# A sparse-attention and MoE kernel: another order for the lead-in, finer weight pieces, batch 2's loads behind a gate

## The chip, the cores and the metric

One core of one Trainium2 chip. The metric is the device time of one execution in microseconds.

## What is computed

Four batches of 8 heads, 768 positions, 64 values a head. Every query sees the keys less than 16 positions away, and one key a block of 32 positions (the block's maximum, with the block's mean as its value):

```python
k_sum = k.reshape(B, H, nb, block, D).max(axis=3)
v_sum = v.reshape(B, H, nb, block, D).mean(axis=3)
scores_l = np.where(mask_l, scale * q @ k.T, -1e9)            # |i - j| < 16
scores_s = scale * q @ k_sum.T + np.log(block)
a = softmax(concatenate([scores_l, scores_s]))
x = a @ concatenate([v, v_sum])                               # -> (3072, 512)
h = x @ w_in                                                  # (512, 2048)
out = (h * sigmoid(1.702 * h)) @ w_out                        # (2048, 512)
```

Inputs and output are float32; the kernel works in bf16 and fp16 and accumulates in float32.

## The kernel before

The kernel runs as a sequence of stages on TensorE (PE), written out by hand; each engine's instructions keep the order of the program text.

**The lead-in** does the first half (384 positions) of batch 0's attention with a layout of its own. Keys of head pairs 0 and 1 come over SyncE's queue and are cast on ScalarE (`cast_k0`); all other loads are cast on the way and are issued by GpSimd, in the order of the text: queries of four heads at a time (`load_q0`), keys of pairs 2 and 3, values `v0n`, then w_in in five pieces, w_out in four (512 KB each in SBUF), and the late half of batch 0's queries (`load_q1`). Each of GpSimd's loads first waits for the landing of the eighth load before it. For each pair p the steps are: `k_turn` and `q_turn` (transposes on PE), `k_own` and `q_copy` (out of PSUM), `k_max` (block maxima `ks`, on VectorE), `s_bias` (a band of -30000 outside the window, as a product), `s_own` and `s_edges` (scores), `s_exp`; for two pairs at once `b_turn` and `b_exp` (block scores). `v_sum` forms block sums of values with products by shifted selector matrices `E`. `av_own`, `av_edges`, `av_blocks` multiply by the values, `v_norm` divides, `x_turn` and `x_copy` give the transposed x, and `ff_first` begins the first two column tiles of the first product. `idle` issues products whose result is not used.

**Stages behind it.** `ff_in(u)` multiplies half u of x by w_in, 128 columns at a time, and ScalarE applies the gelu into `gT`. `ff_out(u, ms, part)` multiplies by w_out, 128 tokens (`ms`) and four of the 16 row tiles at a time; its 12 slots are numbered, and tables `plan0` (batch 0's second half beside the first `ff_out`) and `plan1` (batch 1 beside the second) say which attention step follows which slot: q = `q_late`, t = `tq` (query transposes), s = `scores` (products and exp), m = `mask` (VectorE multiplies by the 0/1 mask `mk`), v = `values`, x = `tx`. Batches 1 to 3 then go through a loop in which the two products use seven block products instead of eight, on sums and differences of weights (`ws`, by `w_sum`) and of `gT` (`gs`).

**Loads of the batches.** `load_batch(b)` issues, on GpSimd, four key loads (192 KB each), twelve value loads (64 KB each) and the query loads of batch b. For batch 2 it stands in the text after slot 2 of the second `ff_out`; GpSimd gets to it whenever it has done what stands ahead. `value_rows(s)` copies halo rows of the values (SyncE's queue), sums them by blocks on PE (`vsum`, tile `ps_vs`) and spreads the sums (`vw<-vs`). `xk` and `xq` turn keys and queries by DMA on SyncE's queue.

Of the kernel before, what the change touches and what calls it, by code (L numbers as in the profile page):

```python
# [35 lines left out]
def kernel(  # L36
# [47 lines left out]
    RQ = 4  # L84
# [13 lines left out]
    def cast_k0(p):  # L98
        if p == 0:
            kb2[0] = castp2.tile([128, 4, RK, D], BF16, name="kb", tag="kb")  # L100
        act.activation(out=kb2[0][:, 2 * p:2 * p + 2].rearrange("p h r d -> p h (r d)"), in_=k0f[p], func=ACT.Copy)
# [82 lines left out]
    mk = consts.tile([128, NQ, QT], BF16, name="mk")  # L184

    def masks():
        pool.memset(mk[:, 2:4], 1.0)
        for par, own, blk, halo in ((0, 0, 64, 96), (1, 64, 0, 32)):
            mid = 2 + par
# [42 lines left out]
    def clear_values(eng, s):  # L232
        eng.memset(vw[s][96:128, 0], 0.0)
        eng.memset(vw[s][96:128, 0, :, D:VC], 1.0)
        eng.memset(vw[s][32:64, NQ - 1], 0.0)
        eng.memset(vw[s][32:64, NQ - 1, :, D:VC], 1.0)
# [25 lines left out]
    def load_w_out(c):  # L262
        wo = moe_w_out.rearrange("(nt ni) d -> ni nt d", ni=128)
        pool.dma_start(out=w_out_sb[:, c * 4:(c + 1) * 4, :],
                       in_=wo[:, c * 4:(c + 1) * 4, :])
# [32 lines left out]
    def idle(n, cols=128):  # L298
# [82 lines left out]
    def k_turn(p):  # L381
        ps = st["K", p] = pturn.tile([128, 1024], BF16, name="ps_k", tag="turn")
        o = 2 * (p % 2)
        turn_plain(ps[:, 0:S], kb2[p // 2][:, o:o + 2])
# [16 lines left out]
    def q_turn(p):  # L401
        if p % 2 == 0:
            st["Q2"] = pturn.tile([128, 1024], BF16, name="ps_q", tag="turn")
        st["Q", p] = st["Q2"][:, p % 2 * HALF:p % 2 * HALF + HALF]
        turn_plain(st["Q", p], qe[:, 2 * p:2 * p + 2])
# [11 lines left out]
    def q_late(p, eng):  # L417
        if p < 2:
            ps = psb.tile([128, 2048], BF16, name="ps_q", tag="big")
        else:  # L420
            ps = pmm.tile([128, 1024], BF16, name="ps_q", tag="mm")
        turn_plain(ps[:, 0:HALF], qb2["late"][:, 2 * p:2 * p + 2])
        copy(eng, qT[p][0][:, HALF:S].rearrange("p (c r) -> p c r", r=JH),
             ps[:, 0:HALF].rearrange("p (r c) -> p c r", r=JH))
# [58 lines left out]
    def v_sum(ps_):  # L483

        for p in ps_:
            if p == 0:
                t = pturn.tile([128, 512], F32, name="ps_vt", tag="turn")
                st["VT", 0], st["VT", 1] = t[:, 0:2 * D], t[:, 2 * D:4 * D]
                st["VT", 0, 1] = t[:, 0:4 * D]
            elif p > 1:  # L490
                st["VT", p] = pturn.tile([128, 512], F32, name="ps_vt", tag="turn")[:, 0:2 * D]
            for i in range(2):
                for j in range(NJ):
                    o = EX - (p % 2 * 2 + i) * 32 - 4 * j
                    pe.matmul(out=st["VT", p][:, i * D:(i + 1) * D], lhsT=E[:, o:o + 128],
                              rhs=v0n[:, 2 * p + i, j, 0:D],
                              start=(j == 0), stop=(j == NJ - 1), skip_group_check=True)

    def v_copy(ps_, eng):
        h0, n = 2 * ps_[0], 2 * len(ps_)  # L500
        copy(eng, vs4[:, h0:h0 + n, 0:D], st[("VT",) + ps_].rearrange("p (h d) -> p h d", d=D))
# [94 lines left out]
    def mask(half, p):  # L596
        a = a_sb[half, p]
        dve.tensor_mul(a, a, mk[:, half * TH:(half + 1) * TH, :].unsqueeze(1)
                       .to_broadcast([128, 2, TH, QT]))
# [269 lines left out]
    def ff_out(u, ms, part):  # L869
        if part == 0:  # L870
            po_now[ms] = pmm.tile([128, d_model], F32, name="po", tag="mm")
        po = po_now[ms]
        for nt in range(4 * part, 4 * part + 4):
            pe.matmul(out=po, lhsT=gT[u % 2][:, nt, ms * 128:(ms + 1) * 128],
                      rhs=w_out_sb[:, nt, :], start=(nt == 0), stop=(nt == NT - 1))
        if part == 3:
# [7 lines left out]
    gate3 = consts.tile([128, 2], F32, name="gate3")  # L884
    dve.memset(gate, 0.0)

    def gelu_soon():

        act.activation(out=gate[:, 1:2], in_=gate[:, 0:1], func=ACT.Gelu_apprx_sigmoid)
# [5 lines left out]
    dve.memset(warm, 0.0)  # L895
# [25 lines left out]
    bands()  # L921
    dve.memset(v0n[:, :, :, D:VC], 1.0)
    clear_sums(dve)
    dve.tensor_copy(out=ident16, in_=ident)
# [11 lines left out]
    s_bias(1)  # L936
    q_copy(0, dve)
    q_copy(1, dve)
    k_max(0)
    idle(8)  # L940
    s_own(0)
    s_own(1)
    s_edges(0)
    s_exp(0)
    s_edges(1)
    s_exp(1)
    k_max(1)
    k_turn(2)
    k_own(2, dve)
    b_turn(0)  # L950
    k_turn(3)
    k_own(3, act)
    b_exp(0)
    q_turn(2)
    q_turn(3)
    q_copy(2, dve)
    q_copy(3, dve)
    k_max(2)
    k_max(3)
    s_bias(2)  # L960
    s_bias(3)
    s_own(2)
    s_own(3)
    s_edges(2)
    s_exp(2)
    s_edges(3)
# [8 lines left out]
    av_edges(0)  # L975
# [5 lines left out]
    v_sum((2,))  # L981
    v_copy((2,), act)
# [4 lines left out]
    v_sum((3,))  # L987
    v_copy((3,), act)
# [11 lines left out]
    gelu_soon()  # L1000
    x_turn(3)
    ff_first(1)
    x_copy(3, dve)
    ff_first(2)
    ff_first(3)
# [7 lines left out]
    dve.memset(vw[0][:, :, :, D:VC], 1.0)  # L1013
# [11 lines left out]
    dve.memset(vw[1][:, :, :, D:VC], 1.0)  # L1025
# [69 lines left out]
    for i, (ms, part) in enumerate((ms, part) for part in range(4) for ms in range(JH)):  # L1095
        ff_out(0, ms, part)
        beside0(i)
        if i in (10, 11):
            w_sum(i - 10, 0)
            w_sum(i - 10, 1)  # L1100

    todo = {3: [lambda: tk(0, 1, act)], 4: [lambda: w_sum(2, 0)], 5: [lambda: tk(1, 1, act)],
            6: [lambda: w_sum(2, 1)], 7: [lambda: w_sum(3, 0)], 8: [lambda: tk(2, 1, act)], 
            10: [lambda: w_sum(3, 1)], 9: [lambda: tq(0, 1, dve)], 11: [lambda: tk(3, 1, act)], 12: [lambda: tq(1, 1, dve)],
# [8 lines left out]
    for i, (ms, part) in enumerate((ms, part) for ms in range(JH) for part in range(4)):  # L1113
        ff_out(1, ms, part)
        beside(1, i)
        if i == 2:
            load_batch(2)
# [5 lines left out]
    for b in range(1, B - 1):  # L1123
# [5 lines left out]
        for n in range(0, NT, 2):  # L1129
# [12 lines left out]
            if nxt:  # L1142
                if n == 0 and b > 1:
# [112 lines left out]
```

## Time and profile before

| | |
|---|---|
| Time, median of 3 runs | 205.96 us (205.91 to 206.78) |
| The profiled execution's own time | 205.39 us |
| Its span, first to last instruction | 203.4 us |
| PE / VectorE / ScalarE / GpSimd busy | 196.7 / 141.2 / 125.4 / 89.9 us |
| Mean granted PE clock | 0.998 |
| DMA packets moved | 28.13 MB, mean 138 GB/s |
| GpSimd's DMA queue (`software_dynamic`) | 69648 packets, 84.8% of 16 engines' span |

The busy times are unions of an engine's instructions. A matmul's end is modelled, so a full PE means that none of its waits is seen, not that it is at its peak. In a chain of waits each piece shows start, length and what was running; a DMA's time to landing runs from its issue. In tables by stretch the columns are the stretch, its length, the busy time of each engine with its count of instructions, the granted PE clock, the DMA engines' mean concurrency and the GB/s that they moved. Rows name instructions as engine, operation, out<-in, shape and count; all have line 28, that of a helper, so tiles tell them apart.

### The profile page before, as it was taken

What the parts mean: (1) busy time and instruction counts of PE and PEld (TensorE: products, weight loads), DVE (VectorE), ACT (ScalarE), POOL (GpSimd) and SP (SyncE); (2) the same over time, 40 slices, a digit from 0 to 9 for tenths busy, and PEclk for the clock granted to TensorE, in tenths of its full rate; (3) what the DMA queues carried; (4) which work ended last, traced back from release to release, by engine and by line L of the source; (5) the groups of instructions that cost most, each with busy time, mean ns of one, the idle gap of its engine ahead of it and who ended that gap; (6) DMA issues with size and microseconds to landing.
All of it is one profiled execution on the core that took longest, in us unless ns stands there. A gap on an engine that the chain in (4) does not pass through costs nothing.

```text
span 203.4 us, 5851 instructions
## 1 busy us (share of the span) xinstructions
PE 196.7 (97%) x2358; PEld 136.6 (67%) x2358; DVE 141.2 (69%) x391; ACT 125.4 (62%) x240; POOL 89.9 (44%) x141
## 2 busy tenths in 40 slices
PE   6889999999999999999999999999999999999993
PEld 5548655556754566655888876666888865578882
DVE  6586894694856884898767789896769567758221
ACT  4584976638786717777871446778670559984220
POOL 7964489447899584000986034000000009980000
PEclk9999999999999999999999999999999999999999
DMA  5999999999999999999999979999022930000223
GB/s 171 169 165 204 207 207 215 189 156 243 116 122 170 176 170 178 127 165 155 114 181 156 173 140 139 110 247 179 0 104 62 185 119 3 0 0 0 106 105 103
DMA packets 95994, 28.13 MB, mean 138 GB/s; under 512 B 83664, under 2 KB 93152, under 8 KB 95968
## 3 DMA queue, kind: packets, MB, share of 16 engines
q0 software_dynamic: 69648, 13.24, 84.8%
q1 hardware_dynamic: 26176, 14.39, 34.8%
q8 instruction: 18, 0.29, 0.6%
q10 hardware_dynamic: 144, 0.13, 0.2%
q14 instruction: 8, 0.07, 0.1%
HBM read 27.26 MB, written 6.29 MB: 165 GB/s over the span
## 4 chain that ended last, share of the span: by engine, by line
PE 91%; DMA 3%; DVE 3%; issue 1%; ACT 0%; POOLq 0%; DVEq 0%
PE ph L28 32%; PE poA L28 16%; PE po L28 11%; PE poB L28 7%; PE phA L28 4%; PE ps_av L28 4%; PE poC L28 4%; PE ps_s L28 3%; DMA qe<-in_q_dram 3%; DVE ks L28 2%; PE ps_t L28 1%; PE ps_x L28 1%; PE phC L28 1%; PE phB L28 1%; PE phE L28 1%; DVE qT L28 1%
## 5 line engine op out<-in xcount | busy, mean ns | idle before, releaser
L28 PE MATMUL ph<-xT,w_in_sb 128*128 128x384 f16 x400 | 67.8, 326 | 0.1
L28 PEld LDWEIGHTS <-w_in_sb 128*128 128x128 f16 x442 | 42.7, 98 | 27.2 <-issue 0.2
L28 ACT ACTIVATE gT<-ph 128x384 f16<-128x384 f32 x100 | 47.9, 491 | 18.4 <-PE ph L28 17.6
L28 PEld LDWEIGHTS <-gT 128*128 128x128 f16 x312 | 28.8, 98 | 11.3 <-issue 0.2
L28 ACT ACTIVATE a_sb<-ps_s 128x768 bf16<-128x768 f32 (+1 forms) x32 | 25.0, 826 | 12.0 <-PE ps_s L28 12.0
L28 PEld LDWEIGHTS <-gs 128*128 128x128 f16 x288 | 27.7, 98 | 3.4
L28 POOL DMA_DIRECT2D vw<-in_v_dram x36 | 24.6, 699 | 11.9 <-DMA kb<-in_k_dram 5.4
L28 POOL TENSOR_TENSOR gs<-gT 128x384 f16<-128x384 f16 x8 | 7.3, 911 | 43.3 <-ACT gT L28 43.2
L28 PE MATMUL po<-w_out_sb,gT 128*128 128x512 f16 x96 | 23.6, 380 | 0.0
L28 PE MATMUL poA<-ws,gs 128*128 128x256 f16 x144 | 18.7, 273 | 0.0
L28 DVE TENSOR_TENSOR a_sb<-a_sb,mk 128x768 bf16<-128x768 bf16 x28 | 14.9, 554 | 5.5 <-ACT a_sb L28 5.0
L28 DVE TENSOR_TENSOR x<-ps_av,rc 128x384 f16<-128x384 f32 x32 | 17.8, 557 | 1.1
L28 DVE TENSOR_TENSOR gs<-gT 128x384 f16<-128x384 f16 (+1 forms) x34 | 13.3, 390 | 7.2 <-ACT gT L28 6.9
L28 POOL DMA_DIRECT2D qb<-in_q_dram x16 | 15.1, 961 | 2.5 <-DMA w_in_sb<-in_moe_w_in_dram 1.2
L28 PEld LDWEIGHTS <-kx 64*128 64x128 bf16 (+1 forms) x378 | 9.9, 95 | 6.8 <-issue 3.6
L28 POOL DMA_DIRECT2D kb<-in_k_dram x14 | 13.6, 986 | 0.3 <-issue 0.3
L28 DVE TENSOR_REDUCE ks<-kx 128x24 bf16<-128x768 bf16 x12 | 11.4, 948 | 3.4 <-ACT kx L28 3.2
L28 ACT ACT_TABLE_LOAD x10 | 12.8, 1283 | 1.0 <-PEq L1240 0.8
L28 ACT ACTIVATE osb<-poA 128x256 f32<-128x256 f32 x9 | 3.5, 384 | 16.1 <-PE poA L28 16.1
L28 ACT ACTIVATE s<-poA 128x256 f32<-128x256 f32 x11 | 4.2, 385 | 11.2 <-PE poA L28 11.2
L28 PEld LDWEIGHTS <-a_sb 128*64 128x64 bf16 (+2 forms) x400 | 7.9, 108 | 2.8 <-issue 1.3
L28 PE MATMUL poA<-ws,gT 128*128 128x256 f16 x72 | 9.3, 273 | 0.0
(117 smaller groups left out, 288.2 us busy)
## 6 DMA issues: line engine op xcount, KB each, us to landing
out_dram<-osb SPq DMA_DIRECT2D x22, 256.0 KB, 3.9
kb<-in_k_dram POOLq DMA_DIRECT2D x14, 192.0 KB, 6.6
qb<-in_q_dram POOLq DMA_DIRECT2D x12, 192.0 KB, 10.5
vw<-in_v_dram POOLq DMA_DIRECT2D x36, 64.0 KB, 5.5
w_out_sb<-in_moe_w_out_dram POOLq DMA_DIRECT2D x4, 512.0 KB, 12.8
w_in_sb<-in_moe_w_in_dram POOLq DMA_DIRECT2D x3, 512.0 KB, 12.4
vw<-vs SPq DMA_DIRECT2D x6, 198.0 KB, 6.6
gT<-in_k_dram SPq DMA_DIRECT2D x2, 384.0 KB, 3.4
```

Source lines behind the costliest of these rows:

```text
L28: r = f(*a, **kw)
```

## The change

- The first four heads' queries come in two loads of two heads instead of one of four, and with three rows a partition (128 partitions) instead of four (96); the identity is built between them. Each pair's `q_turn` has its own PSUM tile.
- Keys of pairs 0 and 1 are cast into a layout that full 128 x 128 transposes can take.
- `idle`: 28, 4 and 8 bf16 products of 128 columns become 4 of 256 columns and 2 of 128 in float32.
- The block sums of the first four heads are one group of 6 products (`v_sum4`) with a second selector `E4`, then multiplied by a 0/1 tile `own`; `selectors` sets both tiles, and the clearing of `v0n`, `ks0` and `vs4` moves ahead of `bands`.
- The order of the lead-in: scores of a pair are followed at once by its edges and exp; `k_own(0)` moves from ScalarE to VectorE, `q_copy(3)` from VectorE to ScalarE; the first pair's products and `v_sum4` move ahead of `b_turn(1)`; `ff_first(1)` ahead of `x_turn(3)`.
- One mask of two tiles for all positions instead of one for every tile; rows outside the sequence are zero in `vw` now, the ones column too.
- w_in in seven pieces instead of five; w_out in eight (row tiles 0-2, 2-4, 4-6, 6-8, 8-12, 12-14, 14-16) rather than four, with the masks behind the third of them.
- The first `ff_out` takes two row tiles a step (24 slots); `plan0` is renumbered and `q_late` does two pairs at once. In `plan1` both t steps follow slot 2 and s02, s03 follow slot 3.
- `w_sum` moves later; its last two parts go into batch 1's loop.
- `load_batch(2)` stands after slot 3, and GpSimd first copies one column of the tile that the exp of pair 2 (s02) writes.

The diff, cut:

```diff
-    RQ = 4
+    RQ = 3
...
-    def load_q0(g):
-        pool.dma_start(out=qe[:, 4 * g:4 * g + 4].rearrange("p h r d -> p h (r d)"),
-                       in_=q[0, 4 * g:4 * g + 4, 0:HALF].rearrange("h (p r) d -> p h (r d)", r=RQ))
+    def load_q0(a, z):
+        pool.dma_start(out=qe[:, 2 * a:2 * z].rearrange("p h r d -> p h (r d)"),
+                       in_=q[0, 2 * a:2 * z, 0:HALF].rearrange("h (p r) d -> p h (r d)", r=RQ))
...
+    E4 = lead.tile([128, 20 + 128], BF16, name="E4")
+    own = lead.tile([128, 4, 1], F32, name="own")
-    warm = lead.tile([128, 512], BF16, name="warm")
+    warm = lead.tile([128, 256], F32, name="warm")
...
     def selectors():
         dve.memset(E, 0.0)
+        dve.memset(E4, 0.0)
+        dve.memset(own, 0.0)
         for g in range(4):
             dve.memset(E[32 * g:32 * g + 32, EX + g:EX + g + 1], 1.0)
+            dve.memset(E4[32 * g:32 * g + 32, 20 + g:20 + g + 97:32], 1.0)
+            dve.memset(own[32 * g:32 * g + 32, g], 1.0)
...
-    mk = consts.tile([128, NQ, QT], BF16, name="mk")
+    mk = consts.tile([128, 2, QT], BF16, name="mk")
...
-    def finish_masks():
-        masks()
-
-        for t in (0, 4, 6, 8, 10):
-            pool.tensor_copy(out=mk[:, t:t + 2, :], in_=mk[:, 2:4, :])
-        pool.memset(mk[96:112, 0, :], 0.0)
-        sel(mk[32:64, NQ - 1, :], 15, 0, -1)
...
     def load_batch(b):
+        if b == 2:
+            pool.tensor_copy(out=gate2, in_=a_sb[0, 2][:, 0, 0, 0:1])
...
+    def v_sum4():
+
+        ps = pturn.tile([128, 512], F32, name="ps_vt", tag="turn")[:, 0:4 * D].rearrange("p (h d) -> p h d", d=D)
+        for j in range(NJ):
+            pe.matmul(out=ps, lhsT=E4[:, 20 - 4 * j:148 - 4 * j], rhs=v0n[:, 0:4, j, 0:D],
+                      start=(j == 0), stop=(j == NJ - 1), skip_group_check=True)
+        dve.tensor_mul(vs4[:, 0:4, 0:D], ps, own.to_broadcast([128, 4, D]))
...
-    load_q0(0)
+    load_q0(0, 1)
     identity()
+    load_q0(1, 2)
     load_k0(2)
     load_k0(3)
-    load_q0(1)
+    load_q0(2, 4)
...
-    for n0, n1 in ((0, 256), (256, 512), (512, 1024), (1024, 1536), (1536, 2048)):
+    for n0, n1 in ((0, 256), (256, 512), (512, 768), (768, 1024), (1024, 1280), (1280, 1536), (1536, 2048)):
...
-    load_w_out(0)
+    load_w_out(0, 2)
+    load_w_out(2, 4)
     for a in range(NP):
         load_q1(a)
-    for c in range(1, 3):
-        load_w_out(c)
-    finish_masks()
-    load_w_out(3)
+    load_w_out(4, 6)
+    masks()
+    load_w_out(6, 8)
+    load_w_out(8, 12)
+    load_w_out(12, 14)
+    load_w_out(14, 16)
...
-    idle(28)
+    idle(4, 256)
     k_turn(0)
-    k_own(0, act)
+    k_own(0, dve)
+    idle(2, 128)
     s_bias(0)
-    idle(4)
+    q_turn(0)
     k_turn(1)
     k_own(1, act)
-    q_turn(0)
+    q_copy(0, dve)
+    s_bias(1)
     q_turn(1)
...
-    v_sum((0,))
+    av_own(0)
+    av_edges(0)
+    v_sum4()
+    dve.tensor_copy(out=ident16, in_=ident)
     b_turn(1)
     b_exp(1)
-    v_sum((1,))
-    v_copy((0, 1), dve)
-    av_own(0)
     av_own(1)
...
-    plan0 = {1: ["q0", "q1", "q2"], 2: ["s0", "s1", "q3", "m0", "m1"], 4: ["s2", "s3", "m2", "m3"], 6: ["v0", "v1"], 8: ["x0"], 9: ["x1"]}
+    plan0 = {5: ["q0", "q2"], 8: ["s0", "s1", "m0", "m1"], 11: ["s2", "s3", "m2", "m3"], 17: ["v0", "v1"],
+             20: ["x0"], 23: ["x1"]}
-    plan1 = {-1: ["s00", "s01"], 1: ["t2", "m00", "m01"], 2: ["t3", "s02"], 3: ["s03", "m02"], 4: ["m03", "s10"],
+    plan1 = {-1: ["s00", "s01"], 1: ["m00", "m01"], 2: ["t2", "t3"], 3: ["s02", "s03"], 4: ["m02", "m03", "s10"],
...
-    for i, (ms, part) in enumerate((ms, part) for part in range(4) for ms in range(JH)):
-        ff_out(0, ms, part)
+    for i, (ms, a) in enumerate((ms, a) for a in range(0, NT, 2) for ms in range(JH)):
+        ff_out(0, ms, a, a + 2)
         beside0(i)
...
-        if i == 2:
+        if i == 3:
             load_batch(2)
...
+                if b == 1 and n in (8, 10):
+                    w_sum(3, n // 2 - 4)
```

More of the change, by code (lines that the diff above doesn't have):

```diff
@@ L260, in load_w_in, with load_w_out @@
         pool.dma_start(out=w_in_sb[:, :, n0:n1], in_=wi[:, :, n0:n1])
-    def load_w_out(c):
+    def load_w_out(a, z):
         wo = moe_w_out.rearrange("(nt ni) d -> ni nt d", ni=128)
-        pool.dma_start(out=w_out_sb[:, c * 4:(c + 1) * 4, :],
-                       in_=wo[:, c * 4:(c + 1) * 4, :])
+        pool.dma_start(out=w_out_sb[:, a:z, :], in_=wo[:, a:z, :])
     def copy(eng, out, in_):
@@ L296, in vsum, with idle @@
                               start=(j == 0), stop=(j == NJ - 1), skip_group_check=True)
-    def idle(n, cols=128):
+    def idle(n, cols):
         for i in range(n):
@@ L401, in q_turn @@
     def q_turn(p):
-        if p % 2 == 0:
-            st["Q2"] = pturn.tile([128, 1024], BF16, name="ps_q", tag="turn")
-        st["Q", p] = st["Q2"][:, p % 2 * HALF:p % 2 * HALF + HALF]
+        st["Q", p] = pturn.tile([128, 1024], BF16, name="ps_q", tag="turn")[:, 0:HALF]
         turn_plain(st["Q", p], qe[:, 2 * p:2 * p + 2])
@@ L417, in q_late @@
     def q_late(p, eng):
-        if p < 2:
-            ps = psb.tile([128, 2048], BF16, name="ps_q", tag="big")
-        else:
[L421 to L424, printed above, removed]
+        if p == 0:
+            big, step = psb.tile([128, 2048], BF16, name="ps_q", tag="big"), 1024
+        else:
+            big, step = pmm.tile([128, 1024], BF16, name="ps_q", tag="mm"), HALF
+        both = [big[:, o:o + HALF] for o in (0, step)]
+        for i, ps in enumerate(both):
+            turn_plain(ps, qb2["late"][:, 2 * (p + i):2 * (p + i) + 2])
+        for i, ps in enumerate(both):
+            copy(eng, qT[p + i][0][:, HALF:S].rearrange("p (c r) -> p c r", r=JH),
+                 ps.rearrange("p (r c) -> p c r", r=JH))
     def s_bias(p):
@@ L481, in score_tiles, with v_sum @@
                           rhs=qT[p][s][r, i * QT:i * QT + QT], start=True, stop=True)
[L483 to L501, printed above, removed]
+    def v_sum4():
[4 more added lines that the diff above has]
+        dve.tensor_mul(vs4[:, 0:4, 0:D], ps, own.to_broadcast([128, 4, D]))
+    def v_sum(p):
+        ps = pturn.tile([128, 512], F32, name="ps_vt", tag="turn")[:, 0:2 * D]
+        for i in range(2):
+            for j in range(NJ):
+                o = EX - (p % 2 * 2 + i) * 32 - 4 * j
+                pe.matmul(out=ps[:, i * D:(i + 1) * D], lhsT=E[:, o:o + 128], rhs=v0n[:, 2 * p + i, j, 0:D],
+                          start=(j == 0), stop=(j == NJ - 1), skip_group_check=True)
+        copy(act, vs4[:, 2 * p:2 * p + 2, 0:D], ps.rearrange("p (h d) -> p h d", d=D))
     def pv_of(p):
@@ L867, with ff_out @@
     po_now = {}
-    def ff_out(u, ms, part):
-        if part == 0:
+    def ff_out(u, ms, a, z):
+        if a == 0:
             po_now[ms] = pmm.tile([128, d_model], F32, name="po", tag="mm")
         po = po_now[ms]
-        for nt in range(4 * part, 4 * part + 4):
+        for nt in range(a, z):
             pe.matmul(out=po, lhsT=gT[u % 2][:, nt, ms * 128:(ms + 1) * 128],
                       rhs=w_out_sb[:, nt, :], start=(nt == 0), stop=(nt == NT - 1))
-        if part == 3:
+        if z == NT:
             osb = outp.tile([128, d_model], F32, name="osb", tag="osb")
@@ L884 @@
     gate3 = consts.tile([128, 2], F32, name="gate3")
+    dve.memset(warm, 0.0)
     dve.memset(gate, 0.0)
@@ L980 @@
     v_norm(1)
-    v_sum((2,))
-    v_copy((2,), act)
+    v_sum(2)
     av_own(2)
```

72 lines of the change are left out of this document (31 added, 41 removed).

## The prediction

> **What bounds the kernel now.** I read the page's busy times first, then the chain of waits, then TensorE's own waits behind the lead-in.
>
> ```profile
> PE 196.7 (97%) x2358; PEld 136.6 (67%) x2358; DVE 141.2 (69%) x391; ACT 125.4 (62%) x240; POOL 89.9 (44%) x141
> ```
>
> The chain of waits in order of time, up to the first dense stretch (start, length, what):
>
> ```profile
> 1.38 6.09 DMA qe<-in_q_dram
> 7.51 0.55 PE ps_q L28 x16
> 8.09 1.02 DVE qT L28 x2
> 9.11 1.73 DVE ks L28 x2
> 12.06 1.02 DVE qT L28 x2
> 13.08 1.73 DVE ks L28 x2
> 15.66 1.30 PE ps_av L28 x38
> 17.33 0.75 PE ps_av L28 x19
> 20.59 10.07 PE ph L28 x62
> ```
>
> TensorE's waits from 20.6 us to the end of the span: the answer is its heading alone.
>
> ```profile
> engine line waited for: us in total, times, longest us
> ```
>
> So there are two kernels in one. Up to about 20.4 us the chain runs through the query load and VectorE (copies qT, block maxima ks). From there TensorE never waits. A shorter lead-in therefore ends the kernel earlier by as much, but only where whatever feeds TensorE later was early enough to spare it. That is the question of each step below.
>
> **The change, part by part. The lead-in.** Rows of its timeline:
>
> ```profile
> 1.35 0.57 DVE L28 MEMSET E<- 128x122 uint32 x5
> ...
> 2.67 0.28 DVE L28 TENSOR_TENSOR band<-wide 128x223 bf16<-128x223 bf16 x1 [0.75 <-POOL wide L28]
> ...
> 4.46 0.66 DVE L28 COPY bias<-band 128x384 bf16<-128x384 bf16 x3
> ...
> 10.74 0.95 DVE L28 COPY qT<-ps_k 128x768 bf16<-128x768 bf16 x1
> ...
> 16.45 0.52 PE L28 MATMUL ps_av<-vs,ab 128*128 128x130 bf16 x6
> ...
> 20.25 0.34 PE L28 MATMUL ps_x<-ident,x 128*128 128x128 f16 x3
> ```
>
> Queries: the first load carries half the bytes and lands, by half of about 1.2 us of data, near 6.9 instead of 7.47; the second pair near 7.6. VectorE has more to do ahead of that. Selector memsets go from 5 to 15 (0.11 each by the row, so +1.1), and about 0.7 of clearing now stands ahead of the bands, whose work (2.67 to 5.12) takes 2.45. Five old memsets end at 1.92, so the bias is ready near 1.92 + 1.1 + 0.7 + 2.45 = 6.2, not 5.12, and the first key copy, now on VectorE, ends at 7.1. All of it lies beside the query load, which covers it by about 0.3 us; without that cover it would cost up to 1 us.
>
> Then VectorE's queue sets the pace: query copies at 7.4 and 8.4 (0.5 each), maximum 0 to 9.85, key copy 2 (0.95) to 10.9, maximum 1 to 11.75, query copy 2 to 12.25 (copy 3 is now ScalarE's), maxima 2 and 3 to 14.0. Before, the last maximum ended at 14.81: 0.8 gained. Behind it TensorE did block scores, a value sum and both pairs' products before the block products at 16.45, 1.64 us later. The new order has half of that done already (one sum for four heads, first pair's products), leaving about 0.9: block products near 14.9, 1.5 earlier. From there to the last transpose (20.25) TensorE's work is the same. The last copy is no longer covered by a second product, about -0.2. Lead-in gain X = 1.3 us; from 0.5 (if the 1.1 us of memsets surfaces) to 1.8.
>
> The idle products shrink from 40 to 6 in another type. They stand in waits; cost 0 unless the clock falls, which is 1.00 in every window row below.
>
> **Weights.** The second stage must have its rows of w_out. DMA rates of two stretches (two 256 KB pieces, three 512 KB pieces; last column GB/s), then the third w_out load's issue and its time to landing, then the products around it:
>
> ```profile
> 14.30:16.90 2.60, 2.21 (x58) 1.76 (x57) 1.00 (x3) 1.63 (x3) 1.43 (x3) 1.00 1.53 194
> 17.00:24.60 7.60, 7.53 (x101) 5.19 (x98) 6.02 (x24) 5.71 (x13) 3.16 (x5) 1.00 1.25 206
> ```
>
> ```profile
> 23.59 0.76 POOL L28 DMA_DIRECT2D w_out_sb<-in_moe_w_out_dram  x1 [1.46 <-DMA w_in_sb<-in_moe_w_in_dram]
> ```
>
> ```profile
> w_out_sb<-in_moe_w_out_dram POOLq DMA_DIRECT2D x1, 512.0 KB, 13.4
> ```
>
> ```profile
> 36.95 1.90 PE L28 MATMUL po<-w_out_sb,gT 128*128 128x512 f16 x8
> ```
>
> That load lands at 23.59 + 13.4 = 36.99. Its first user is the fifth of those eight products, at 36.95 + 0.87 = 37.82: 0.83 us of slack. The queue is full all the way (194 to 206 GB/s), so it sets when the load lands. The change leaves this load whole (steps 8 to 12), with the same bytes ahead of it, the same 24 products and the same query and score work ahead of its user. Finer w_in pieces cost 1 MB at 194 instead of 206, 0.3 us; halo and sum rows that now come earlier may take up to 0.3 more or nothing. So of X = 1.3 only G = 0.83 - 0.3 = 0.5 passes, the rest becomes a wait at step 8; bounds 0.0 and 0.85. The smaller pieces elsewhere only remove waits that were not there.
>
> The Trainium skill, "DMA: Bandwidth & Descriptors", section "Anatomy of one DMA", fits a load at about 2.0 us plus its bytes over 436 GB/s, and so speaks against splitting: five more loads ahead of step 8 would be an estimated 10 us there. The rows above (194 against 206 GB/s) show next to none of it, since loads follow each other without a gap.
>
> The one mask takes five copies, a memset and a select off GpSimd ahead of w_out's last quarter, which is not late; VectorE's mask products keep their element count: 0. The w_out differences move on VectorE, two of them (0.7 each) into the next stage: 0 to +0.3, taken 0. The last transpose of the first output stage now comes at its end: 0 to +0.2, taken 0.
>
> **Batch 2's loads held.** GpSimd now waits for the exp of pair 2 before it issues 4 key, 12 value and 4 query loads; all of these stand behind that wait, and the block sums of batch 2 on TensorE need the last value load. The rows: batch 2's key loads, its last value load with time to landing, the exp, and the block sums.
>
> ```profile
> 58.86 4.04 POOL L28 DMA_DIRECT2D kb<-in_k_dram  x4
> ```
>
> ```profile
> 73.58 0.70 POOL L28 DMA_DIRECT2D vw<-in_v_dram  x1
> ```
>
> ```profile
> vw<-in_v_dram POOLq DMA_DIRECT2D x1, 64.0 KB, 6.4
> ```
>
> ```profile
> 61.91 0.81 ACT L28 ACTIVATE a_sb<-ps_s 128x768 bf16<-128x768 f32 x1 [1.23 <-PE ps_s L28]
> ```
>
> ```profile
> 80.26 0.60 PE L28 MATMUL ps_vs<-vw,E 64*32 64x128 bf16 x48
> ```
>
> The last value load lands at 73.58 + 6.4 = 79.98 and is used within 80.26 to 80.79: next to no slack. The exp ended at 62.72. One slot later (four products, 0.87) and G = 0.5 earlier it ends at 63.1: the loads start at 63.2, 4.3 us later than at 58.86. How long they then take has two ends in the trace. Batch 2 took 79.98 - 58.86 = 21.1 us beside other transfers. Batch 3's same 16 loads:
>
> ```profile
> 96.38 1.02 POOL L28 DMA_DIRECT2D kb<-in_k_dram  x1 [0.32 <-issue]
> ```
>
> ```profile
> kb<-in_k_dram POOLq DMA_DIRECT2D x1, 192.0 KB, 4.2
> ```
>
> ```profile
> 109.13 0.72 POOL L28 DMA_DIRECT2D vw<-in_v_dram  x1
> ```
>
> ```profile
> vw<-in_v_dram POOLq DMA_DIRECT2D x1, 64.0 KB, 3.0
> ```
>
> took 109.13 + 3.0 - 96.38 = 15.7. Batch 2's split, by its last key load, and the rate of such loads in a stretch with nothing beside them:
>
> ```profile
> 61.87 1.04 POOL L28 DMA_DIRECT2D kb<-in_k_dram  x1
> ```
>
> ```profile
> kb<-in_k_dram POOLq DMA_DIRECT2D x1, 192.0 KB, 7.8
> ```
>
> ```profile
> 38.50:43.50 5.00, 5.00 (x77) 2.99 (x76) 4.05 (x11) 2.00 (x3) 1.93 (x3) 1.00 2.42 159
> ```
>
> Keys were down at 61.87 + 7.8 = 69.67 after 10.8 us, values 10.3 us later. Held, the keys no longer meet the sum rows and the first store: 4.2 for the first, three more at 192 KB by 159 GB/s (1.24), so 7.9. The values meet the same stores and key transposes as before, because TensorE times those too: 10.3. Together 18.2, nearer the batch's own row than batch 3's. Last landing 63.2 + 18.2 = 81.4. The sums over the loads that landed sooner are done by then, so the stage ends near 81.55 instead of 80.79: +0.8 us, in which the 0.5 of G is spent already. Ends: 15.7 lands at 78.9, in time, -0.5; 21.1 lands at 84.3, +3.7. Nothing behind that stage has slack to give back.
>
> **Sum.** The profiled execution took 205.39 (span 203.4 and 2.0 around it). X = -1.3, of which the weight stream takes back 0.8 (G = -0.5), and the held loads turn -0.5 into +0.8: 206.2. The median of the runs shown, 205.96, is 0.57 above that execution, so **206.8 us**.
>
> **Rivals.** *The held loads land in time* (nearer batch 3's 15.7 us, up to about 17): G stays, 205.96 - 0.5 = 205.4, 204.9 to 205.9. For it: the queue is empty when they start. Against: the stores and key transposes that batch 2 met stay where TensorE's progress puts them. *The held loads are later still* (the other side, slower): the third store and the second key transposes fall among the values, at 20 us or more: landing 83.2 to 84.3, +2.6 to +3.7, about 208.6 (207.7 to 209.7); it decides from 18.5 us on, where 206.99 is passed. For it: these transposes are issued at 75.63, TensorE's progress times them, and the values now still flow then.
>
> ```profile
> 75.63 3.76 SPq L28 DMA_TRANSPOSE kx<-kb  x2
> ```
>
> *The weights keep up* and the loads are in time: X whole, 205.96 - 1.3 = 204.7. Against: the full queue. *Each load pays its fixed part in the stream* (the skill's rule): 256 KB loads would land a good 2 us apart beyond their data, step 8 starts some 9 us late, about 215; the rates speak against it. *The change doesn't do what it says*, no shorter lead-in: G = 0, the gate 0.5 later, 207.3.
>
> **Numbers.** About 0.5% (1.03 us) can be told from no change, so the lines are 204.93 and 206.99. Forecast (206.0 to 207.7) 0.44, of it 0.16 beyond 206.99; in time 0.28, of it 0.02 below 204.93; later still 0.16; weights keep up 0.06; no shorter lead-in 0.04, beyond the line; fixed part 0.02. Slower 0.16 + 0.16 + 0.04 + 0.02 = 0.38; faster 0.02 + 0.06 = 0.08; same 0.54. The range, 205.0 to 208.3, leaves out about a tenth on either side; the likeliest case's own is 206.0 to 207.7.
>
> **What would show it.** In the changed kernel: the last x transpose near 19 instead of 20.25; a TensorE wait of 0.5 to 1 us for w_out's third quarter near 36 to 37; the first batch 2 key load issued near 63; a TensorE wait of about 1.3 us at ps_vs, released by a value load. If that wait is missing, the held-loads step is wrong and the time is near 205.4; if the x transpose is still beyond 20, the lead-in step is.

## The result, and the profile after

The changed kernel took 215.78 us (median of 6 runs, 213.99 to 216.95), the kernel before 206.37 beside it (205.5 to 207.43): 1.0449 times as long, 95% interval 1.0386 to 1.0512. Forecast were 206.8 and 205.0 to 208.3. The profiled execution took 216.95 us, span 214.8; the account below is made against it and against the 203.4 of before. Of one experiment (the exp one slot sooner, first run) the profiled execution had a lower clock from end to end (0.854, 228.79 us), so only the times of its other three are used.

The page: busy times, and the granted clock in 40 slices.

```profile
PE 201.7 (94%) x2292; PEld 137.5 (64%) x2292; DVE 141.8 (66%) x397; ACT 124.7 (58%) x240; POOL 93.5 (44%) x141
...
PEclk9999999999999998569999999999999999999999
```

PE was full 97% of a shorter span before. It now has 13 us in which no product runs (6.7 before), and three slices (8, 5 and 6 tenths) in which its clock is down. Its waits from 20 us on, where there were none before:

```profile
engine line waited for: us in total, times, longest us
PE ps_vs L28 <- DMA vw<-in_v_dram: 6.2, 6, 1.9
PE po L28 <- DMA w_out_sb<-in_moe_w_out_dram: 1.4, 2, 1.1
PE ph L28 <- DMA w_in_sb<-in_moe_w_in_dram: 0.3, 1, 0.3
PE phC L28 <- DVE phC L28: 0.2, 1, 0.2
```

The place of the loss, PE's timeline at batch 2's value sums (before: one row, 0.60 us at 80.26, then 96 products in 15.77):

```profile
81.21 0.34 PE L28 MATMUL ps_vs<-vw,E 64*32 64x128 bf16 x17
...
84.93 0.31 PE L28 MATMUL ps_vs<-vw,E 64*32 64x128 bf16 x7 [1.52 <-DMA vw<-in_v_dram]
87.09 0.26 PE L28 MATMUL ps_vs<-vw,E 64*32 64x128 bf16 x1 [1.85 <-DMA vw<-in_v_dram]
...
89.55 10.66 PE L28 MATMUL ph<-xT,w_in_sb 128*128 128x384 f16 x49
```

And by stretch (length, then busy PE, PEld, DVE, ACT, POOL; clock; DMA concurrency; GB/s):

```profile
81.00:84.40 3.40, 1.01 (x27) 0.36 (x26) 2.08 (x7) 0.65 (x2) 2.40 (x3) 1.00 1.62 197
84.40:89.50 5.10, 1.32 (x23) 0.54 (x22) 0.00 (x0) 0.00 (x0) 1.67 (x2) 0.51 2.31 111
89.50:94.70 5.20, 5.20 (x24) 2.47 (x18) 1.43 (x5) 1.47 (x3) 0.00 (x0) 0.50 2.47 160
94.70:100.00 5.30, 5.30 (x34) 3.21 (x33) 4.51 (x14) 3.92 (x8) 0.00 (x0) 1.00 1.20 191
```

The sums start 0.95 us later than before (81.21 against 80.26), and the products behind them 8.8 later (89.55 against 80.79). The first 49 of these take 10.66 us, half of it at half clock; at the pace of before (15.77 for 96) they take 8.05: 2.6 more. 8.8 + 2.6 = 11.4, the whole difference of the spans. From 100 us on next to nothing differs: one wait of 0.2 us.

Why the values are late: the first of the held loads and its time to landing, and the last value load.

```profile
65.47 1.02 POOL L28 DMA_DIRECT2D kb<-in_k_dram  x1 [0.30 <-PE ps_s L28]
...
78.97 0.68 POOL L28 DMA_DIRECT2D vw<-in_v_dram  x1
```

```profile
vw<-in_v_dram POOLq DMA_DIRECT2D x1, 64.0 KB, 10.3
```

Issued from 65.47 (58.86 before), down at 78.97 + 10.3 = 89.27: 23.8 us for the same 16 loads that took 21.1 before. What stands beside them on SyncE's queue, and what ScalarE did ahead of the exp that the gate waits for:

```profile
71.62 3.74 SPq L28 DMA_TRANSPOSE kx<-kb  x2
76.07 0.34 SPq L28 DMA_DIRECT2D out_dram<-osb  x1
76.58 3.99 SPq L28 DMA_TRANSPOSE kx<-kb  x2
```

```profile
63.62 0.60 ACT L28 ACTIVATE osb<-po 128x512 f32<-128x512 f32 x1 [1.86 <-issue]
64.12 2.21 ACT L28 ACTIVATE a_sb<-ps_s 128x768 bf16<-128x768 f32 x3
```

Both pairs of key transposes are issued before the last value load is; before, the second pair was issued at 75.63, when the last value load (73.58) was already on its way. And the score of pair 2, moved from slot 2 to slot 3 of `plan1`, now stands behind a stage that begins 1.1 us later (59.24 against 58.16), one slot, and an output copy.

The lead-in and the weights:

```profile
12.15 1.80 DVE L28 TENSOR_REDUCE ks<-qT 128x24 bf16<-128x768 bf16 x2
...
15.38 0.52 PE L28 MATMUL ps_av<-vs,ab 128*128 128x130 bf16 x6
...
19.41 0.33 PE L28 MATMUL ps_x<-ident,x 128*128 128x128 f16 x3
...
29.79 0.76 POOL L28 DMA_DIRECT2D w_out_sb<-in_moe_w_out_dram  x1
...
38.91 2.75 PE L28 MATMUL po<-w_out_sb,gT 128*128 128x512 f16 x12 [1.15 <-DMA w_out_sb<-in_moe_w_out_dram]
```

```profile
w_out_sb<-in_moe_w_out_dram POOLq DMA_DIRECT2D x1, 512.0 KB, 9.1
```

The lead-in ends 0.84 us sooner. w_out's third quarter lands at 29.79 + 9.1 = 38.9, 1.9 later than before, and PE waits for it.

### The profile page after: what moved, and what is told of

It reads as the page before. It is cut to its first block, busy times and chain, and to the rows that moved or that the text cites. A ratio compares the mean times of both kernels' runs of the same rounds, so it can differ in the third digit from the quotient of the medians.

```text
span 214.8 us, 5728 instructions
## 1 busy us (share of the span) xinstructions
PE 201.7 (94%) x2292; PEld 137.5 (64%) x2292; DVE 141.8 (66%) x397; ACT 124.7 (58%) x240; POOL 93.5 (44%) x141
## 5 line engine op out<-in xcount | busy, mean ns | idle before, releaser
L28 PE MATMUL ph<-xT,w_in_sb 128*128 128x384 f16 x400 | 70.7, 334 | 0.5 <-DMA w_in_sb<-in_moe_w_in_dram 0.3
L28 PEld LDWEIGHTS <-w_in_sb 128*128 128x128 f16 x442 | 43.4, 100 | 29.9 <-issue 3.7
L28 DVE TENSOR_TENSOR a_sb<-a_sb,mk 128x768 bf16<-128x768 bf16 x28 | 14.9, 554 | 7.4 <-ACT a_sb L28 4.8
L28 DVE TENSOR_REDUCE ks<-kx 128x24 bf16<-128x768 bf16 x12 | 11.4, 947 | 3.0 <-ACT kx L28 2.9
L28 PE MATMUL poA<-w_out_sb,gT 128*128 128x256 f16 x72 | 9.4, 273 | 0.0
```

The lines of the kernel that those rows point to most:

```text
L28: r = f(*a, **kw)
```

## Experiments

Theory A: the hold costs nearly everything, in waits at the value sums and in the clock. Rival B: the weights and the lead-in cost much of it. Starts and landings below are of the profiled executions.

### Without the hold; the hold alone

```diff
# e1, on the changed kernel          # e2: the same lines added to the kernel before
-        if b == 2:
-            pool.tensor_copy(out=gate2, in_=a_sb[0, 2][:, 0, 0, 0:1])
-        if i == 3:
+        if i == 2:
             load_batch(2)
```

> The changed kernel without the hold: no copy on GpSimd ahead of batch 2's loads, and they are issued behind the third product group as before. Theory A (the hold costs nearly all: TensorE waits 6.2 us in batch 2's value sums, and its clock is halved for 10.2 us around them): about 207.3 us, the kernel before plus the 0.95 us by which the changed kernel already stood later ahead of the held loads; the sums (ps_vs) take about 0.6 us, granted clock near 1.00 throughout. Rival B (the weight stream and the lead-in lose time of their own beyond what is seen at 81 us, or lower the clock): 210 us or more.

> The kernel before with the hold alone (the copy on GpSimd that waits for the exp of pair 2, and the loads one product group later). Theory A: about 214 to 216 us, 8 to 10 above the kernel before, with the same two signs, waits of some 6 us in the value sums and a halved clock behind them. Rival B: at most 3 us above the kernel before, and a clock near 1.00.

Without the hold 205.81 us, before 205.81: ratio 0.9993 (0.9964 to 1.0022). The hold alone on the kernel before: 211.82, ratio 1.0288 (1.0261 to 1.0315). PE's waits from 20 us on, without the hold and then with the hold alone:

```profile
PE po L28 <- DMA w_out_sb<-in_moe_w_out_dram: 1.0, 1, 1.0
```

```profile
PE ps_vs L28 <- DMA vw<-in_v_dram: 3.9, 4, 1.2
PE phC L28 <- DVE phC L28: 0.2, 1, 0.2
```

Theory A holds: the rest of the change together makes no difference that these runs can tell (less than 0.8 us either way by the interval). Two things were not as expected: without the hold it was 1.5 us better than theory A said, and the hold alone cost 6 us, not 8 to 10, against 10 in the changed kernel.

### The hold kept, the sums later

```diff
-                if n // 2 == 1:
+                if n // 2 == (4 if b == 1 else 1):
                     value_rows(s)
```

> The changed kernel with the hold, but batch 2's value rows (halo rows, value sums, sum rows) come three steps of two tiles later in the first feed-forward stage, about 10.5 us, so behind the last landing (89.27 us in the changed kernel). Theory A: the loads land as late as in the changed kernel, but TensorE has other products meanwhile: ps_vs waits under 0.5 us, clock near 1.00, about 207 us. Rival C (other users of the held loads are as late: key transposes, query copies, or the value rows' own transfers become late for the products that use them): 209 to 213 us, with waits at ps_s or ps_o behind the sums.

206.71 us, ratio 1.0040 (1.0021 to 1.0059). The loads start at 64.44 and the last of them lands at 85.7, still 5.8 us later than before, but the sums stand at 88 and wait for nothing:

```profile
87.97 0.60 PE L28 MATMUL ps_vs<-vw,E 64*32 64x128 bf16 x48
```

So the late loads cost about 9 us only through the one place that uses them.

### Products in the waits

```diff
# e4: behind steps 1 to 4 of the six     # e8: ahead of steps 3, 4, 5: 18, 18, 6, start=False
+  for _ in range(4):
+      pe.matmul(out=ps[0][:, 2*D:512], lhsT=w_in_sb[:, 0, 0:128], rhs=w_in_sb[:, 1, 0:512-2*D], start=True, ...)
```

> The changed kernel with 40 products that nobody uses (4 of 384 columns behind each of 10 steps of batch 2's value sums, 0.16 us each), so that TensorE is busy in most of its waits. The landings don't change. If the clock is a cost by itself (theory A: of the loss some 2.6 us lie in products at half clock behind the sums, up to 4 with the sums themselves): granted clock stays near 1.00, the stretch from 81.2 us ends at 89.5 as before, and the whole is 212 to 213.5 us. Rival: short waits are not what lowers the clock: half clock for some 10 us again, and 215.5 to 217 us.

> The earlier kernel with filler products was weaker than its text said: the sums have six steps of two loads each, so it got 16 products, not 40. Here 42 unused products of 384 columns (18, 18 and 6 ahead of the last three steps, 6.8 us at 0.162 us each) fill nearly all of the 6.2 us that TensorE waits in batch 2's value sums; the landings don't change. Theory A (half the clock is a cost of its own): granted clock at 0.998, the sums end near 89.6 us as in the changed kernel, 49 products behind them take 8.0 instead of 10.7 us: 2.5 to 3 us under the changed kernel's profiled execution, some 213 to 214 us. Rival (the clock falls for another reason than idle time): 0.975 to 0.984 again and 215.5 us or more.

In the first (16 products; with start=True they disturb batch 2's block sums in the same bank) the mean clock was 0.992 instead of 0.975 to 0.984, so some 3.4 us at half clock (2 x 0.008 of the span). It took 214.87 us. In the second it was 0.999 to 1.000 in all four runs, and the time 214.83 us. By stretch:

```profile
81.00:84.40 3.40, 2.26 (x37) 1.36 (x36) 1.82 (x7) 0.49 (x1) 2.51 (x3) 1.00 1.64 187
84.40:91.50 7.10, 6.05 (x56) 3.19 (x54) 0.00 (x0) 0.00 (x0) 2.02 (x2) 1.00 2.56 118
91.50:107.00 15.50, 15.50 (x103) 9.31 (x96) 13.34 (x46) 11.09 (x23) 4.42 (x6) 1.00 1.44 137
```

So idle time at the sums is what lowers the clock: with PE busy 2.26 of the first 3.4 us it stays, with 1.01 it falls. Both kernels are 0.9 us under the changed kernel in the median, not the 2 to 3.5 expected, and that is less than the runs of the changed kernel scatter (214.0 to 217.0). In the second the products behind the sums ran at full pace, but the sums ended 2.0 us later, with 3.1 and 1.2 us of unused products right ahead of the last two steps. The clock's 2.6 us is therefore read from the rows; as a difference of times it is not shown.

### The transposes beside the loads

```diff
# e6: both pairs; e11: g = 1 alone
-        if i in (9, 11):
-            xk(i // 2 - 4, 0)
...
                 if n // 2 == 1:
                     value_rows(s)
+                    if b == 1: xk(0, s); xk(1, s)
# e6 also: rest_k two steps later for b == 1
# e7: as e6, and load_v(2) ahead of load_turned(k, 2)
```

> The changed kernel with the hold, but both pairs of batch 2's key transposes are issued behind the halo and sum rows of the value sums, and the key rows (block maxima) two steps later. Theory E (the transposes, four of some 2 us of issue each, fall among the held value loads and are what stretches them from the 18.2 us forecast to 23.8): the last value load lands 18 to 19 us after the first issue, near 84 us; the waits at ps_vs fall from 6.2 us to 1.5 to 2.5, about 208.5 to 210 us if the transposes are in time for the scores behind. Rival F (the value loads are slow by themselves, or by the stores and rows beside them): still 22 us or more, 214 to 216 us.

> The changed kernel with the hold; only the second pair of batch 2's key transposes is moved behind the value sums, the first pair stays where it was. With both pairs among the held loads the last value landed 23.8 us after the first issue, with none 16.7. Theory E (each pair stretches the loads by its own part, so the forecast of 18.2 us, which counted one pair as in the kernel before, missed the second): about 18 to 20.5 us, last landing near 84 us, waits at ps_vs of 2 to 3 us, 209.5 to 212 us. Rival (the first pair alone does the harm): 22 us or more.

> As the kernel with the later transposes, and the held batch loads its values ahead of its keys. The value loads then have 10 to 11 us by the kernel before's split (10.3 us for the values), so land near 76 us, well ahead of the sums at 81: no wait at ps_vs, clock near 1.00. If that is all, about 206.5 us. If keys that land near 84 us are late for their transposes and block maxima (rival), a wait of 1 to 3 us appears at the scores near 96.5 us: 207.5 to 210.

With no transposes among them the loads went from 64.29 to 77.62 + 3.4 = 81.02, in 16.7 us:

```profile
64.29 1.02 POOL L28 DMA_DIRECT2D kb<-in_k_dram  x1 [0.31 <-PE ps_s L28]
...
77.62 0.73 POOL L28 DMA_DIRECT2D vw<-in_v_dram  x1
```

```profile
vw<-in_v_dram POOLq DMA_DIRECT2D x1, 64.0 KB, 3.4
```

With the first pair alone 21.2 us (63.87 to 85.07; waits of 4.0 us), with both 23.8. The values differ most: behind the last key load's landing they need 6.3 us with no transposes (74.67 to 81.02), 10.5 with one pair and 13.4 with both. The keys take 10.4 to 10.7 in all three.

That the transposes stretch the loads is shown. The kernel with the later sums started its loads within 0.2 us of this one (64.44), with both pairs among them, and took 21.3 us for 16.7. The third store stood among the loads in both (75.03 and 74.89), so it is not what makes the difference. From 76 to 84 us GpSimd's queue moved 0.51 MB in the kernel with the later sums, 0.37 in the changed kernel and 0.81 without the transposes.

That each pair adds a part of its own is not shown. With both pairs among them the loads took 19.5 to 23.9 us in the other traces at full clock, with the first alone 21.2, and the values' part with both pairs was only 10.5 and 10.6 us in the two traces with the exp sooner (below).

The times were 210.73 (ratio 1.0262), 212.24 (1.0321) and, with the values first, 212.26 us (1.0323). In the last the values were down at 76.2, with no wait at the sums, but what was moved came late elsewhere. PE's longest waits in the first of these:

```profile
PE poA L28 <- DVE s L28: 1.9, 1, 1.9
PE poB L28 <- DVE gs L28: 0.8, 1, 0.8
PE ps_vs L28 <- DMA vw<-in_v_dram: 0.5, 1, 0.5
```

VectorE does the key rows in its order, and the copies and differences that the next products need stand behind them. With the values first PE waits in the same two places (2.0 and 1.0 us), and the clock then falls for 3.4 us in both kernels. So the price is that of the moved transposes and key rows. The rival of the third expectation, keys that are late because they are loaded last, is not shown: the scores that it named waited 0.8 us, and for queries.

### Why 10 us here and 6 on the kernel before

```diff
# e13, e15, e18 on the changed kernel    # e14: gate on a_sb[0, 1], loads at i == 2
-  plan1 = {..., 2: ["t2", "t3"], 3: ["s02", "s03"], ...
+  plan1 = {..., 2: ["t2", "t3", "s02"], 3: ["s03"], ...
```

> The changed kernel with the hold; only the score of pair 2 in batch 1's early half stands one slot sooner, as in the kernel before, so that its exp runs on ScalarE ahead of the output copy of the first store and not behind it (in the changed kernel that copy runs at 63.6 and the exp that the loads wait for at 64.1 us). Theory I (the order on ScalarE and the slot started the loads 1.5 us too late, and each us of start costs more than one, since both key transposes then fall among the values): first key load near 64 us, last value landing near 85.5 to 87, 211.5 to 213.5 us. Rival (the start time doesn't matter, only that the loads are held): 215 to 216.5 us.

> The changed kernel with the hold shortened: the loads are issued behind the third product group as before, and wait for the exp of pair 1, not pair 2. Their first issue comes near 62 us, between the kernel without the hold (59.4) and the hold on the kernel before (63.4). Theory I: last value landing 82 to 83.5 us, TensorE waits 1 to 2.5 us, no or one window at half clock, 207 to 209 us. Rival (any hold gives the whole loss): 211 us or more.

The shorter hold took 207.25 us (ratio 1.0081, 1.0052 to 1.0109): start 61.78, landing 81.3, a wait of 0.7. The earlier exp took 214.0 to 216.6. It was run again, on another chip, and then a third time on one chip beside the changed kernel and the hold alone:

> The kernel with the exp one slot sooner once more, since the profiled execution of its first run had a lower clock from start to end and shows no landings. The times of that run, 214.0 to 216.6, already lie above what theory I asked for (211.5 to 213.5). Theory I survives only if the trace shows the loads starting as late as in the changed kernel, 65 us or more, so that the earlier exp did not start them earlier. Rival: first key load near 64 us and a landing of 88 us or more all the same: then something else than the start makes the difference to the hold alone (63.36 us, landing 84.98).

> The changed kernel itself, beside the next two kernels on one chip, since the kernel with the exp one slot sooner took 214.0 to 216.6 us on one chip and 207.7 to 209.5 on another. Theory I (the start of the held loads decides): first key load near 65.3 us, last value landing 88 to 89.5 us, 214 to 216 us, so above both others. Rival J (how fast the chip moves the loads decides, and the starts make little): within 1.5 us of the other two, whatever the level.

> The kernel before with the hold alone, on the same chip as the changed kernel. Theory I: first key load near 63.4 us, landing near 85 us, 211 to 212.5 us, 3 us or more below the changed kernel. Rival J: within 1.5 us of the changed kernel.

> The changed kernel with the exp of pair 2 one slot sooner, on the same chip. Theory I: first key load near 64 us, landing 83 to 86 us, 208 to 212.5 us, 3 us or more below the changed kernel. Rival J: within 1.5 us of the changed kernel.

On the second chip the earlier exp took 207.7 to 209.5 (and 213.0 once). On the third, 209.61 (207.9 to 211.0) beside 212.11 for the hold alone (211.7 to 214.0) and 215.40 for the changed kernel (213.3 to 216.5). ScalarE with the exp sooner, that the loads wait for, and the last value load, on the third chip:

```profile
62.57 0.81 ACT L28 ACTIVATE a_sb<-ps_s 128x768 bf16<-128x768 f32 x1 [1.71 <-PE ps_s L28]
63.59 0.60 ACT L28 ACTIVATE osb<-po 128x512 f32<-128x512 f32 x1 [0.21 <-PE po L28]
```

```profile
vw<-in_v_dram POOLq DMA_DIRECT2D x1, 64.0 KB, 7.5
```

In the table the stage is the second `ff_out`, by its first product. The rows "again" and "third run" are of the third chip.

| kernel (profiled execution) | stage begins | first issue | last landing | us | wait at ps_vs | mean clock |
|---|---|---|---|---|---|---|
| no hold | 58.31 | 59.42 | 79.3 | 19.9 | 0 | 0.998 |
| hold to pair 1's exp | 58.12 | 61.78 | 81.3 | 19.5 | 0.7 | 1.000 |
| hold alone, kernel before | 57.64 | 63.36 | 85.0 | 21.6 | 3.9 | 0.992 |
| hold alone, again | 57.71 | 63.42 | 84.6 | 21.2 | 3.5 | 0.992 |
| exp sooner, second run | 57.96 | 63.81 | 83.3 | 19.5 | 1.5 | 0.999 |
| exp sooner, third run | 58.34 | 63.93 | 83.8 | 19.8 | 1.9 | 1.000 |
| changed kernel | 59.24 | 65.47 | 89.3 | 23.8 | 6.2 | 0.975 |
| changed kernel, again | 59.77 | 66.00 | 89.8 | 23.8 | 6.5 | 0.984 |

On that chip the times are as theory I forecast them, and rival J falls: one score a slot sooner is worth 5.8 us in the median, the runs of the two kernels do not overlap, and its loads land 6 us sooner, with the clock up. That the start of the loads decides is not shown. Of the 2.1 us between the two starts (66.00 and 63.93) 1.4 lie in the stage, which began sooner before the edit could act; behind the stage's start the slot is worth 0.6 us (5.6 against 6.2). And the hold alone starts sooner than the third run, lands later and is slower; its sums also stand 1.1 us sooner. How so little of a start makes 4 us of loads stays open, and so does why the same kernel took 214 us and more on the first chip.

### The weights

```diff
# e5, e12 on e1: w_in (512, 1024), (1024, 1536); e5: w_out 0-4, 4-8, 8-12, masks, 12-16
# e12: w_out 0-4, 4-6, 6-8, 8-12, masks, 12-16
# e9 on e1: plan0 11: [..., "v0"], 17: ["v1"]
# e10 on e1: RQ = 4; load_q0(0, 2), load_q0(2, 4)
```

> The changed kernel without the hold, and with the weights loaded as before: w_in in five pieces, w_out in quarters, the mask work ahead of the last quarter (the first output stage keeps its finer steps). Theory D (the finer pieces are why the third w_out load lands at 37.9 us without the hold where 37.0 was forecast from the kernel before): it lands near 37.0, TensorE's wait for it falls from 1.0 to about 0.2 us, and the time is some 0.7 us under that without the hold, about 205.1 us. Rival (the weight stream is late from its start, since the queries' loads and value loads ahead of it end later: w_in's first piece landed 0.6 us later): at most 0.3 us better, w_out near 37.6.

> The changed kernel without the hold, and the first of the two value products of batch 0's late half (24 products, 0.47 us) stands ahead of the first output step that needs w_out's third quarter, not behind it. Without the hold TensorE waited 1.0 us there and the lead-in's gain was given back in that wait. Theory G (the weight stream takes the lead-in's gain, and only there): the wait falls to about 0.5 us, everything behind is 0.4 to 0.5 us earlier, 205.3 to 205.5 us. Rival (the lead-in gains nothing that lasts): no change, 205.8.

> The changed kernel without the hold, with the queries of the early half loaded as before: two loads of four heads, rows in fours (96 partitions, 512 B pieces), not three loads with rows in threes (128 partitions, 384 B). Theory H (the smaller query pieces and the extra load are why the weight stream starts later: w_in's first piece is issued at 9.44 instead of 8.71 us and landed at 16.6 to 17.7 in the runs so far, 16.8 to 17.0 with the queries as before): w_in's first piece lands near 16.9, w_out's third quarter near 37.2, and the wait there falls by 0.6 us; the first scores start some 0.6 us later, which the same wait hides: about 205.5 us. Rival (the stream's start is set by something else): w_in's first piece beyond 17.2 and 206 us or more.

> A version meant to beat both kernels: the changed kernel without the hold, w_in in five pieces as before, w_out in pieces of 4, 2, 2, 4 and 4 tiles, the mask work behind the third-quarter load. With all weights coarse, w_out's third quarter landed 20.0 us after w_in's first piece, as in the kernel before (20.2); with finer pieces 20.5 to 22.4 later. But the coarse second quarter was late by itself: TensorE waited 1.6 us for it at 35.0, which its finer halves (landed near 33.2 and 34.7) would avoid. Theory D': third quarter near 37.3, waits for weights under 0.5 us, 205.2 to 205.5 us. Rival (the smaller gains don't last or the landings scatter by as much): 205.6 to 206.0.

Coarse weights: 205.71 us, ratio 1.0006 (0.9984 to 1.0027). The stream is faster in its trace: the third quarter landed 20.0 us after w_in's first piece, as with the weights of before (20.0 to 20.2), and 20.5 to 22.4 (middle 20.9) in the fourteen traces with all the finer pieces. (w_out's finer loads are seven; the "eight" in the description of the change is a slip, its list is right.) But PE then waits for the second quarter, which is no longer split:

```profile
35.01 1.45 PE L28 MATMUL po<-w_out_sb,gT 128*128 128x512 f16 x6 [1.60 <-DMA w_out_sb<-in_moe_w_out_dram]
```

The values sooner were a loss, 206.89 (1.0070, 1.0045 to 1.0095). The wait moved to an exp:

```profile
39.04 0.64 PE L28 MATMUL ps_av<-vw,a_sb 128*64 128x65 bf16 x24 [0.73 <-ACT a_sb L28]
```

Their PSUM tile is one of the two that the scores just ahead fill, so they waited for that exp; the gain from the reordered product was not to be had there. Queries as before: w_in's first piece at 17.03 as forecast, but w_out's third quarter at 38.0; 205.95 (1.0008, 0.9981 to 1.0035). Theory H falls: that first piece lies among the 16.6 to 17.7 of the kernels with the new queries, and the third quarter came no sooner. Coarse w_in with a split second quarter (20.5 from the first piece to the third quarter): at 26.34 + 11.0 = 37.3, and 205.26 us against 205.64, ratio 0.9981 (0.9960 to 1.0002). The best version found, by less than these runs can tell from nothing.

## Why the prediction was wrong, step by step

**The failed step** is the time of the held loads: "Together 18.2, nearer the batch's own row than batch 3's". It measured 23.8. Two terms of it were mis-sized. The keys were put at 7.9 us because they "no longer meet the sum rows and the first store"; they took 10.4 (65.47 to 75.89), and as long in the kernel without transposes beside them. The values were put at 10.3, since they "meet the same stores and key transposes as before". That was false for the second pair, which was issued 2 us behind the last value load before and 2.4 us ahead of it now; they took 13.4, and 6.3 where both pairs were moved away. How much of it is the second pair's stays open. The upper bound of 21.1 was no bound, since it came from a batch whose value loads were all issued ahead of the second pair. The start was also mis-sized, 65.47 for 63.2: the exp moved with a stage that began 1.1 us later instead of 0.5 sooner, and the copy ahead of it on ScalarE was not counted though the row was there to read. Start + 2.3, keys + 2.5, values + 3.1: the landing at 89.27 for 81.4. The products behind the sums start at 89.55 for 81.55, 8.0 later than forecast; with the clock's 2.6 that is nearly all of the 10.75 us between the forecast for the profiled execution (206.2) and its 216.95.

**Not in the sum at all** was the clock, 2.6 us. The prediction asked about it only for the idle products of the lead-in. A forecast wait should have been followed by that question: does PE stay busy enough to keep its clock?

**The rival that came true** is *later still*, with 0.16. Of its mechanism, second transposes and third store among the values, the moved transposes show that the transposes count, though not the second pair by itself; the store still stood there where the loads took 16.7 us. Its price, 208.6, was too low, because it kept the start at 63.2, took the old 21.1 as the end and left out the clock. The statement that nothing behind has slack was right: the loss is kept to the end.

**Lead-in.** Right in its order: last maximum at 13.95 (14.0 forecast), block products at 15.38 (14.9), last transpose at 19.41 (19). X is 0.84 in this pair of traces, not 1.3, and less over all of them: 18.8 to 20.0 (middle 19.4) in the sixteen traces with this lead-in, 19.7 to 20.3 (middle 19.8) in three with the old one. The idle products cost nothing visible.

**Weights.** The mechanism was right: the wait is at w_out's third quarter and the stream takes the gain back. The size was not: 38.9 for the landing, not some 37.3. Finer pieces cost 0.5 to 2.4 us (middle 0.9) from w_in's first piece on in these traces, not 0.3, and that piece itself came 0.7 later here (0.2 sooner to 0.9 later in the others). So G was -1.1 in the profiled execution instead of +0.5: the second `ff_out` begins at 59.24 for 58.16. In eleven other traces with this lead-in and these weights it begins at 57.6 to 59.8, and in the times without the hold G is none (0.9993). The Trainium skill ("DMA: Bandwidth & Descriptors", section "Anatomy of one DMA") gives a load a fixed part of about 2.0 us. The prediction rightly set that aside for this stream: w_in's first three pieces, 256 KB each, landed at 17.55, 18.84 and 20.18, 1.3 us apart.

**Range and chances.** The range missed by 7.5 us, as its upper end was built on the 21.1. Slower had 0.38.

## To carry to other kernels

A transfer that is moved later does not take its old time with it: list what its new place has beside it, each transpose and store that others time, before taking a duration or a bound from the old place. When a wait is forecast on the engine that is always busy, price the clock behind it too. And where data are late, moving their one user can be cheaper than moving what runs beside them: the later sums brought 9 us back, the moved transposes 5.

## What the runs showed of the hardware

- The clock fell though no wait of PE was longer than 1.9 us (1.2 in the hold alone): 1.01 us busy of 3.40 was little enough (81.0 to 84.4), 2.26 of 3.40 was not. Half clock then lasted from 84.5 to 94.7, with 5.2 us of dense products in it. The Trainium skill, "TensorE: Matmul & The Clock Gate", section "What's actually happening", has the clock halved after an idle window of about 3.4 us and full after a busy one, with windows that run free. The lengths at half clock agree (3.4, 6.8 or 10.2 us), but a window need not be all idle. Cut at the clock's own changes, the 3.41 us ahead of each of the eight falls before the last products held 0.46 to 1.28 us of products, and no stretch with 1.81 us or more was followed by one, in the nineteen traces that reach full clock. It rose behind stretches with 3.14 us or more, and not behind 2.55 and 2.60.
- The same sixteen loads took 16.7 to 23.9 us by what was beside them and when they started; from 76 to 84 us GpSimd's queue moved 0.81 MB without the key transposes and 0.37 to 0.51 MB with both pairs.
- The same kernel (exp one slot sooner) took 207.7 to 211.0 us on two chips (213.0 once) and 214.0 to 216.6 on another, while the medians of the kernel before lay between 205.5 and 206.4 on all of them. What differs between the chips is not known.
